# Moving the crossbar transpose of q behind the transposes of u in SyncE's queue, in a pooled-attention and mixer kernel

## The chip, the cores and the metric

The kernel runs on one core of a Trainium2 chip. The metric is device time in microseconds (us). With one core in use, the time of the slowest core is the time of that core. Before the change the kernel took 353.03 us, the median of three runs (352.23 to 353.3).

For this one-core program a run is called slow when it is over 1.5% above the fastest run of the same kernel. The ratios use fast runs only; a median is quoted over all runs of a kernel, slow ones too.

## The reference

The reference is an attention whose keys and values are averaged over groups of eight rows, followed by a mixer of two small networks. There are 8 batches, 8 heads, 576 rows and 64 columns per head.

```python
k_p = k.reshape(B, H, 72, 8, D).mean(axis=3)          # 576 keys become 72
v_p = v.reshape(B, H, 72, 8, D).mean(axis=3)
attn = softmax(scale * q @ k_p.T)                     # 576 x 72 per head
x = (attn @ v_p)  ->  (B, 576, 512)                   # heads side by side
u = x + (relu(x.T @ w_tok1) @ w_tok2).T               # token network, 576 -> 256 -> 576
out = u + relu(u @ w_ch1) @ w_ch2                     # channel network, 512 -> 1536 -> 512
```

## The kernel before

The kernel is a pipeline over batches. After a head, which does the attention and the token network of batch 0, come the *units*. Unit n is the channel network of batch n, 48 steps of two matmuls each. Between those steps the attention and token network of batch n+1 are mixed in, step by step. Unit 8 handles a ninth row block collected from all batches ("tails").

```python
LATER = {0: "kpT", 2: "o0", 3: "e0", 5: "o1", 6: "e1", 8: "o2", ...        # scores of batch n+1, from step 2
         ..., 26: "at0", 27: "at1", 30: "u0 t0", 31: "u1 t1", 32: "u2 t2", 33: "u3 t3", 34: "u4 t4"}
...
def unit(n, at):
    side = {}
    if n + 1 < B:
        load(n + 2)               # loads of k, q, v for the batch after next
        batches[n + 1][0]()       # prepare(n + 1): pooling of k and v, and the transpose of q
        side = batches[n + 1][1]
    for i, _ in enumerate(unit_steps(n, ...)):
        for s in at.get(i, "").split() if side else []:
            ... side[s]()
```

Each batch needs two kinds of crossbar transposes, both issued by SyncE. *qT* turns q of a batch (a 128 x 2560 bf16 tile, 640 KB) into the layout that the scores need. *uT* turns u (four pieces of 128 KB, steps t0 to t3, and every second batch a fifth piece for the tails) into the layout that the next channel network needs. SyncE also issues the two outputs of each of a unit's four output chunks, at steps 29, 35, 41 and 47, ahead of what else stands at that step.

```python
def load(b):
    kr = raw.tile(...); vr = raw.tile(...)                 # raw has two buffers of each
    qb = raw.tile([P, HP, BR * D + D], BF16, name="qb")
    nc.vector.memset(qb[:, :, BR * D:], 0.0)               # padding, on VectorE, for every batch
    ...                                                    # GpSimd then issues the loads of kr, qb, vr
def prepare():
    ...
    if b > 1:
        for s in ("K0", "K1", "V0", "V1"): name[s]()       # pooling, on GpSimd
    st["qT"] = att.tile([P, HP, NE, 2, BP], BF16, name="qT")
    if not first:
        nc.sync.dma_start_transpose(out=st["qT"]..., in_=qb...)
...
with tc.manual_schedule(engines={PE, POOLE}):              # TensorE and GpSimd: program order
    ...                                                    # SyncE's order is the scheduler's
```

A qb buffer is reused every second batch. Its memset, and with it the next load into it, must wait until the qT that read it has landed.

The softmax here doesn't subtract the row's maximum and nothing guards it: scores larger than these inputs give would overflow.

## Time and profile before

Starts of units are read from the timeline of TensorE: a unit starts with its first channel matmul. All unit lengths in this document are cut that way.

| us | head | unit 0 | 1 | 2 | 3 | 4 | 5 | 6 | 7, 8 and the end | span |
|---|---|---|---|---|---|---|---|---|---|---|
| before | 37.0 | 65.2 | 43.8 | 40.0 | 30.3 | 29.3 | 28.5 | 29.4 | 46.5 | 350.0 |

Units 4 to 6 are bound by TensorE, as unit 5 shows. The table of windows of the kernel before, here its line for unit 5, has for a stretch its length, then the busy time and instruction count of each engine, the granted clock, and the share of the DMA engines' time.

```profile
core 0: us, PE busy (x) PEld busy (x) DVE busy (x) ACT busy (x) POOL busy (x), PEclk, DMA share, GB/s
...
245.70:274.19 28.49, 28.34 (x180) 14.42 (x179) 15.10 (x27) 8.79 (x15) 0.00 (x0) 1.00 0.25 54
```

TensorE is busy for 28.34 of 28.49 us, at a granted clock of 1.00. A unit cannot be much shorter than this, so the time to win is the excess of units 0 to 3, some 65 us over 28.5 each (an estimate that takes unit 5 as the limit of all units).

The page gives the chain that ended last: the critical path followed back from the end, as shares of the span.

```profile
PE 64%; DMA 25%; DVE 7%; SPq 1%; issue 1%; ACT 0%; DVEq 0%; ACTq 0%
DMA qT<-qb 13%; DMA uT<-u 9%; DMA qf<-in_q_dram 2%; DVE o L366 1%; PE p_978 L361 1%; DVE x L255 1%; SPq L316 1%; DVE kTs_93 L198 1%; DVE vp L147 1%; PE p_2923 L361 1%; PE p_2329 L361 1%; PE p_2015 L361 1%; PE p_748 L361 1%; PE p_1923 L361 1
```

The chain passes for 13% of the span through waits for qT and for 9% through waits for uT. The table of waits says which engines stood still for them. The columns are engine, tile and line, what it waited for, us in total, how many times, and the longest.

```profile
PE p_803 L349 <- DMA uT<-u: 11.7, 1, 11.7
...
PE p_1436 L349 <- DMA uT<-u: 8.2, 1, 8.2
PE p_1115 L349 <- DMA uT<-u: 7.6, 1, 7.6
```

The same table for VectorE:

```profile
DVE qb L84 <- DMA qT<-qb: 28.8, 5, 15.9
```

TensorE waits 27.5 us for uT, at the starts of units 1, 2 and 3. VectorE waits 28.8 us in five memsets of qb (line 84). In that time it cannot do the work behind the memset, which TensorE needs.

Why uT is late shows in the issues. Here is SyncE's timeline of the kernel before: start, length, operation; the length is how long the issues occupied the queue.

```profile
84.94 10.66 SPq L316 DMA_TRANSPOSE uT<-u  x4
...
132.26 8.82 SPq L316 DMA_TRANSPOSE uT<-u  x4
...
208.99 5.17 SPq L316 DMA_TRANSPOSE uT<-u  x4
```

GpSimd's timeline has the loads; these two are of batch 6.

```profile
128.41 0.78 POOL L104 DMA_DIRECT2D qb<-in_q_dram  x1
129.18 0.84 POOL L91 DMA_DIRECT2D vr<-in_v_dram  x1
```

At 132.26 the four uT come right behind the loads of batch 6 (kr at 127.56 is the third), at 84.94 right behind those of batch 4 (issued from 83.05 to 85.5), and they keep the queue for 8.82 and 10.66 us. At 208.99, with no loads about, they keep it for 5.17. The landing times say the same. The list of DMA issues, cut to the window from 80 to 104 us, has what was written, the count, the size where it is known, and the median us from issue to landing:

```profile
qb<-in_q_dram POOLq DMA_DIRECT2D x1, 576.0 KB, 13.2
vr<-in_v_dram POOLq DMA_DIRECT2D x1, 576.0 KB, 16.7
uT<-u SPq DMA_TRANSPOSE x4, 12.0
```

And cut to the quiet window from 205 to 216 us:

```profile
uT<-u SPq DMA_TRANSPOSE x4, 2.4
```

A uT lands in 2.4 us when quiet and in 12.0 us beside the loads (both are medians of four). The Trainium skill gives a reason in the page "DMA: Bandwidth & Descriptors", section "Issuing engines are not separate DMA queues": DMAs started by different engines run on the same 16 DMA engines and interleave. This trace agrees, 2.4 against 12.0 us.

SyncE's timeline has seven qT, in the order of the batches: those of batches 1 to 3 from 31.8 to 73.4 us, and those of batches 4 to 7 at 111.71, 155.76, 196.25 and 224.73, each 8 to 10 us into units 1 to 4. That is two units ahead of the scores that read it. The one of batch 6, and then, in TensorE's timeline, the first scores of batch 6, in unit 5:

```profile
196.25 3.11 SPq L171 DMA_TRANSPOSE qT<-qb  x1
...
247.58 0.41 PE L232 MATMUL p_2089<-qT,kTs_92 128*72 128x256 bf16 x2 [0.15 <-DVE kTs_92 L198]
```

These scores run 1.9 us after the start of their unit and 51 us after the issue of their qT; no score waits for a qT in this kernel.

### The profile page before, as it was taken

How to read it: one execution, taken by the hardware profiler on the slowest of the kernel's cores; microseconds unless marked ns; L12 is line 12 of the kernel's file. 1: busy time of each engine (PE TensorE's matmuls, PEld its weight loads, DVE VectorE, ACT ScalarE, POOL GpSimd, SP SyncE). 2: the span in 40 equal slices, each digit the busy share in tenths (PEclk: the TensorE clock that was granted, in tenths of full speed). 3: DMA queues.
4: the chain of work that ended last, by engine and by line, in shares of the span. 5: the costliest groups of instructions: out<-in, count | busy, mean ns of one | idle time of the engine just before them, and what ended most of it. 6: DMA issues, size and time to landing. Idle time of an engine off the chain costs nothing.

```text
span 350.0 us, 4171 instructions
## 1 busy us (share of the span) xinstructions
PE 282.8 (81%) x1632; PEld 139.4 (40%) x1632; DVE 146.8 (42%) x284; ACT 86.1 (25%) x153; POOL 135.5 (39%) x120
## 2 busy tenths in 40 slices
PE   4777806839339498399937999999999999999994
PEld 1453402414115243154413544544554554444441
DVE  3245207834213354126611564465465466332331
ACT  2244602500007100072003600710620450030310
POOL 6491001699999592193805582850000000000000
PEclk9999965978959989699986999999999999999998
DMA  8999999972999929904695316225303502602214
GB/s 189 200 205 204 194 170 130 158 118 34 181 156 150 128 21 185 178 14 62 99 170 131 76 28 132 60 38 105 92 0 62 120 2 45 134 18 63 58 27 95
DMA packets 62067, 37.02 MB, mean 106 GB/s; under 512 B 40416, under 2 KB 56928, under 8 KB 62048
## 3 DMA queue, kind: packets, MB, share of 16 engines
q0 software_dynamic: 20160, 17.35, 32.6%
q1 hardware_dynamic: 41888, 19.41, 30.0%
q8 instruction: 13, 0.21, 0.2%
q14 instruction: 6, 0.05, 0.0%
HBM read 35.85 MB, written 9.44 MB: 129 GB/s over the span
## 4 chain that ended last, share of the span: by engine, by line
PE 64%; DMA 25%; DVE 7%; SPq 1%; issue 1%; ACT 0%; DVEq 0%; ACTq 0%
DMA qT<-qb 13%; DMA uT<-u 9%; DMA qf<-in_q_dram 2%; DVE o L366 1%; PE p_978 L361 1%; DVE x L255 1%; SPq L316 1%; DVE kTs_93 L198 1%; DVE vp L147 1%; PE p_2923 L361 1%; PE p_2329 L361 1%; PE p_2015 L361 1%; PE p_748 L361 1%; PE p_1923 L361 1%; PE p_2580 L361 1%
## 5 line engine op out<-in xcount | busy, mean ns | idle before, releaser
L349 PEld LDWEIGHTS <-w_ch_86 128*128 128x128 bf16 x432 | 41.1, 101 | 63.9 <-issue 32.6
L361 PEld LDWEIGHTS <-GT 128*128 128x128 bf16 x432 | 41.9, 99 | 49.0 <-issue 1.9
L245 PEld LDWEIGHTS <-ex 72*128 72x128 bf16 x320 | 15.2, 99 | 24.1 <-DVE x L255 15.4
L91 POOL DMA_DIRECT2D kr<-in_k_dram x9 | 7.5, 837 | 27.0 <-DVE t_499 L141 26.1
L193 PE MATMUL pt<-ident,kp 72*128 72x72 bf16 x64 | 4.8, 226 | 12.0 <-DVE kp L144 11.3
L84 DVE MEMSET qb<- 128x128 uint32 x8 | 1.3, 165 | 28.8 <-DMA qT<-qb 28.8
L198 DVE COPY kTs_92<-pt 64x576 bf16<-64x576 bf16 (+1 forms) x9 | 3.6, 405 | 22.9 <-PE pt L193 21.9
L349 PE MATMUL p_803<-uT,w_ch_86 128*128 128x512 bf16 x4 | 2.1, 619 | 11.7 <-DMA uT<-u 11.7
L286 PEld LDWEIGHTS <-w_tok_83 128*128 128x128 bf16 x70 | 7.4, 106 | 10.2 <-issue 3.5
L232 PEld LDWEIGHTS <-kTs_93 128*72 128x72 bf16 x64 | 7.3, 118 | 9.3 <-DVE kTs_93 L198 2.6
L232 PEld LDWEIGHTS <-kTs_92 128*72 128x72 bf16 x64 | 7.5, 122 | 8.7 <-DVE kTs_92 L198 2.1
L91 POOL DMA_DIRECT2D vr<-in_v_dram x9 | 7.3, 815 | 9.2 <-DVE t_573 L141 5.8
L193 PEld LDWEIGHTS <-kp 72*128 72x128 bf16 x64 | 4.1, 118 | 16.4 <-DVE kp L144 11.8
L304 PEld LDWEIGHTS <-w_tok_84 128*128 128x128 bf16 x64 | 6.2, 97 | 7.7 <-issue 0.5
L349 PE MATMUL p_1436<-uT,w_ch_86 128*128 128x512 bf16 x4 | 2.1, 619 | 8.2 <-DMA uT<-u 8.2
L349 PE MATMUL p_1115<-uT,w_ch_86 128*128 128x512 bf16 x4 | 2.1, 617 | 7.6 <-DMA uT<-u 7.6
L198 DVE COPY kTs_93<-pt 64x576 bf16<-64x576 bf16 (+1 forms) x10 | 3.9, 394 | 8.5 <-PE pt L193 8.4
L144 POOL TENSOR_TENSOR kp<-t_1725 72x512 bf16<-72x512 f32 x1 | 1.3, 1265 | 14.1 <-PE pt L193 14.1
L144 POOL TENSOR_TENSOR kp<-t_2044 72x512 bf16<-72x512 f32 x1 | 1.3, 1258 | 14.1 <-PE pt L193 14.1
L220 PE MATMUL pt<-ident,qb 128*128 128x128 bf16 x20 | 2.3, 262 | 5.3 <-DVE qT L222 4.7
L354 ACT ACTIVATE GT<-p_803 128x512 bf16<-128x512 f32 x1 | 0.6, 597 | 24.0 <-PE p_803 L349 24.0
L354 ACT ACTIVATE GT<-p_1436 128x512 bf16<-128x512 f32 x1 | 0.6, 597 | 22.7 <-PE p_1436 L349 22.7
(803 smaller groups left out, 703.3 us busy)
## 6 DMA issues: line engine op xcount, KB each, us to landing
out_dram<-o SPq DMA_DIRECT2D x72, 128.0 KB, 2.4
kr<-in_k_dram POOLq DMA_DIRECT2D x7, 576.0 KB, 9.1
qb<-in_q_dram POOLq DMA_DIRECT2D x7, 576.0 KB, 11.8
vr<-in_v_dram POOLq DMA_DIRECT2D x7, 576.0 KB, 15.5
w_ch_86<-in_moe_w_ch_dram POOLq DMA_DIRECT2D x3, 512.0 KB, 9.0
w_ch_87<-in_moe_w_ch_dram POOLq DMA_DIRECT2D x3, 512.0 KB, 18.7
qf<-in_q_dram SPq DMA_DIRECT2D x4, 288.0 KB, 4.1
kr<-in_k_dram POOLq DMA_DIRECT2D x2, 288.0 KB, 9.2
```

The lines of the kernel that those rows point to most:

```text
L91: nc.gpsimd.dma_start(out=t[:, h0:h1].rearrange("j h i d -> j h (i d)"), in_=src[b, h0:h1].rearrange("h (j i) d -> j h (i d)", i=POOL))
L147: eng.tensor_tensor(out=dst, in0=t4[:, 0:n, 0], in1=t4[:, 0:n, 1], op=ALU.add)
L193: nc.tensor.transpose(out=ps[:, h, :], in_=st["kp"][:, h].rearrange("j e d -> j (e d)"), identity=ident[0:SP, 0:SP])
L198: copy(out=kT[rows, half, h0 * SP:h1 * SP], in_=ps[rows, h0:h1, :].rearrange("p h j -> p (h j)"))
L232: nc.tensor.matmul(out=ps[0:SP, hl, 0:n], lhsT=kT[:, odd, h * SP:(h + 1) * SP], rhs=st["qT"][:, hp, 0:n // BP, hl, :], start=True, stop=True)
L245: nc.tensor.matmul(out=ps[:, h // 4, (h % 4) * (D + 1):(h % 4 + 1) * (D + 1)], lhsT=st["ex"][:, h * S + n0:h * S + n0 + P], rhs=st["vp"][: ...
L255: nc.vector.tensor_tensor(out=dst.rearrange("p (a h d) -> p a h d", a=2, d=D)[:, 0:na], in0=view[:, 0:na, :, 0:D], in1=den[rows, 0:na, :, ...
L286: nc.tensor.matmul(out=ps, lhsT=w_tok1[:, CHUNK[c] if c < 4 else 4 + par, m * P:(m + 1) * P], rhs=st["x"][:, c, :] if c < 4 else st["xt"], ...
L304: nc.tensor.matmul(out=ps, lhsT=w, rhs=a, start=(i == 0), stop=(i == len(mms) - 1))
L316: nc.sync.dma_start_transpose(out=dst[:, :, o:o + P], in_=src)
L349: nc.tensor.matmul(out=ps, lhsT=w_ch1[:, kk, m * P:(m + 1) * P], rhs=uT[:, kk, :], start=(kk == 0), stop=(kk == 3))
L361: nc.tensor.matmul(out=ps, lhsT=GT[:, m, c * P:(c + 1) * P], rhs=w_ch2[:, m, :], start=(m == 0), stop=(m == NM - 1))
```

## The change

qT is no longer issued at a place that the scheduler chooses. qT of batch n+2 is now issued at step 38 of unit n, behind uT of that unit and just ahead of its scores, which run from the start of unit n+1, and SyncE works in program order. The intent is that uT, which TensorE needs first, goes ahead of qT, and that qT does not hold up what follows. In unit 0, where t0 to t4 stand at steps 36 to 40, step 38 puts qT between t1 and t2.

```diff
@@ load
+        batches[b][2]["qb"] = qb
+        batches[b][2]["qT"] = att.tile([P, HP, NE, 2, BP], BF16, name="qT")
@@ prepare
-            st["qT"] = att.tile([P, HP, NE, 2, BP], BF16, name="qT")
-            if not first:
-                nc.sync.dma_start_transpose(out=st["qT"]..., in_=qb...)
@@ new
+        def qT_dma():
+            nc.sync.dma_start_transpose(out=st["qT"]..., in_=st["qb"]...)
...
+        name["qx"] = qT_dma
@@ schedule of unit 0: qT of batch 1 at step 4
-    FIRST = {8: "K0", ...
+    FIRST = {4: "qx", 8: "K0", ...
@@ unit
         for i, _ in enumerate(unit_steps(n, batches[n][2] if n < B else None)):
+            if i == 38 and n + 2 < B:
+                batches[n + 2][1]["qx"]()
...
-    with tc.manual_schedule(engines={PE, POOLE}):
+    with tc.manual_schedule(engines={PE, POOLE, SYNC}):
```

The built programs of TensorE, ScalarE and GpSimd are in the same order as before. On VectorE only the memsets of qb move: those of batch 4 and later go from the middle of units 0, 1 and 2 to the end of unit 0 and the starts of units 2, 3 and 4.

## The prediction

> **What bounds it now.** The chain of waits is 64% TensorE and 25% DMA: 13% waits for the q transpose (qT), 9% for the u transposes (uT). Cutting the span (350.0 us) where each unit's first channel matmul starts (timeline): the head takes 37.0, unit 0 65.2, units 1 to 3 43.8, 40.0 and 31.3, units 4 to 6 29.3, 28.4 and 28.7, units 7 and 8 20.7 each, the end 4.9. Units 4 to 6 are TensorE-bound (99% busy); the excess lies in units 0 to 3, about 36 + 15 + 11.5 + 3 us.
>
> Two waits make up most of it:
> - VectorE's memset of a qb buffer stands in front of work that TensorE needs, and waits until the qT that reads that buffer has landed: 15.9 us at 37.8, 1.1 at 60.5, 5.3 at 70.3, 5.2 at 116, 1.3 at 160 (waits of VectorE).
> - uT collides with the next batch's loads. In quiet units uT lands in 2.4 us and four take 5.2 us of queue; at 84.9 to 95.7, beside loads issued at 83.1 to 84.7, the median landing is 12.0 us. TensorE waits 11.7, 7.6 and 8.2 us at the starts of units 1 to 3. The Trainium skill (DMA: Bandwidth & Descriptors, "Issuing engines are not separate DMA queues") says that all queues share 16 engines; these landing times agree.
>
> **What the change does.** No work is added or removed. On SyncE, qT of batch n+2 moves to step 38 of unit n, behind uT (in unit 0 between the second and third uT). The built order shows the later memsets moved to the end of unit 0 and the starts of units 2, 3 and 4. The memset that costs 15.9 us stays, still behind the first qT (31.8 to 53.8, beside weight loads). A qb load waits for the qT that read its buffer, so two of a batch's three loads now start after uT.
>
> **Sum.** Until 60 us nothing changes. Unit 0: the 1.1 and 5.3 us waits go, plus about 2 us of slow matmuls after the second idle; then uT with qT between costs 5 to 7 us of idle: unit 1 starts near 89 instead of 102.3 (-13). Unit 1: the 5.2 and most of 7.6 us go, and slow matmuls after idles (-13). Unit 2: -9. Unit 3: -1. New cost: qT is issued about 26 us into a unit and needs 4.8 us to land when quiet, while the next scores need it at about 30; beside the kr load (22 us into the unit, after 18 us of pooling) it is later. I estimate 0 to 4 us at the starts of units 2 to 6, 6 us in all. Sum: -36 + 6 = -30: span 320; with 2 to 3 us outside it **322 us, range 310 to 334**. Faster by over 2%: 0.95; within 2%: 0.04; slower: 0.01.
>
> **In the profile.** Right if VectorE's wait for qT in the first unit stays near 16 us and the other four almost vanish; TensorE's waits for uT fall from 27.5 us to under 10; unit 0 ends near 89; units 1 to 6 take 28.5 to 33 us; the DMA share of the chain falls to about 12%; new short waits of scores or of the memset for qT at unit starts.
>
> **What would make it wrong.** qT in front of the third uT could cost unit 1's start more than 7 us. qT landing late at every unit could return the gain as a new wait. Or the loads still collide with uT.

Unit 3 is 31.3 us in that text and unit 6 is 28.7, where the table above has 30.3 and 29.4. The sum is the same.

## The result, and the profile after

| kernel | median us | lowest to highest | runs | ratio to before, 95% interval |
|---|---|---|---|---|
| before | 352.63 | 351.18 to 353.3 | 4 | |
| after | 340.72 | 340.39 to 342.8 | 4 | 0.9669 (0.9617 to 0.9721), faster |

A ratio here and below is the mean time of one kernel's fast runs over the mean of the other's fast runs in the same rounds, so it is not quite the ratio of the medians quoted beside it. The result is correct. The gain is 12 us, where 31 were predicted. The direction was right, and the time lies outside the range of 310 to 334.

| us | head | unit 0 | 1 | 2 | 3 | 4 | 5 | 6 | 7, 8 and the end | span |
|---|---|---|---|---|---|---|---|---|---|---|
| before | 37.0 | 65.2 | 43.8 | 40.0 | 30.3 | 29.3 | 28.5 | 29.4 | 46.5 | 350.0 |
| after | 38.9 | 56.3 | 31.0 | 34.8 | 35.1 | 32.8 | 33.1 | 32.6 | 46.4 | 340.9 |
| difference | +1.9 | -8.9 | -12.8 | -5.3 | +4.7 | +3.5 | +4.6 | +3.2 | 0 | -9.1 |

The head varies from 35.6 to 41.7 us over all runs without a pattern, so its +1.9 is not put down to the change. Units 0 to 2 gave 27 us. Units 3 to 6, which had been at or near TensorE's limit, gave 16 back.

The chain of the kernel after, by engine and then by line:

```profile
PE 66%; DMA 19%; DVE 7%; SPq 3%; issue 2%; another core or an unknown queue 1%; ACT 0%; DVEq 0%; ACTq 0%
DMA qT<-qb 14%; DMA uT<-u 3%; DMA qf<-in_q_dram 3%; SPq L373 1%; DVE o L370 1%; DVE x L258 1%; SPq L319 1%; DVE vp L150 1%; PE p_1366 L365 1%; PE p_2923 L365 1%; PE p_1999 L365 1%; PE p_1643 L365 1%; PE p_750 L365 1%; PE p_2549 L365 1%
```

The share of uT fell from 9% to 3%, but that of qT stayed (13% to 14%). The waits of TensorE say what qT does now; waits of 1.9 and 1.1 us for uT are left out here.

```profile
PE p_804 L353 <- DMA uT<-u: 10.2, 1, 10.2
...
PE p_2394 L235 <- DMA qT<-qb: 3.4, 1, 3.4
PE p_1457 L235 <- DMA qT<-qb: 3.0, 1, 3.0
PE p_2090 L235 <- DMA qT<-qb: 3.0, 1, 3.0
PE p_1136 L235 <- DMA qT<-qb: 2.6, 1, 2.6
PE p_1769 L235 <- DMA qT<-qb: 1.9, 1, 1.9
```

And those of VectorE after:

```profile
DVE qb L85 <- DMA qT<-qb: 30.5, 5, 16.1
```

Waits for uT fell from 27.5 to 13.2 us, of which 10.2 is the start of unit 1. But the scores (line 235) of five batches wait for qT, 13.9 us in all, where none did before. VectorE's memsets still wait (30.5 us), at other places.

SyncE's timeline shows the order that the change made. The first three lines are the end of unit 0, the next two that of unit 1 (unit 2 starts at 126.26), and the last four that of unit 4 (unit 5 starts at 228.84).

```profile
79.44 2.55 SPq L319 DMA_TRANSPOSE uT<-u  x2
82.09 4.10 SPq L225 DMA_TRANSPOSE qT<-qb  x1
86.28 2.93 SPq L319 DMA_TRANSPOSE uT<-u  x2
...
118.89 5.17 SPq L319 DMA_TRANSPOSE uT<-u  x4
...
125.44 3.14 SPq L225 DMA_TRANSPOSE qT<-qb  x1
...
220.60 5.18 SPq L319 DMA_TRANSPOSE uT<-u  x4
225.88 1.22 SPq L319 DMA_TRANSPOSE uT_tails<-u_tails  x1
227.19 1.18 SPq L373 DMA_DIRECT2D out_dram<-o  x2
228.46 3.04 SPq L225 DMA_TRANSPOSE qT<-qb  x1
```

And TensorE at the start of unit 5; the bracket gives the wait before an instruction and what ended it.

```profile
229.97 0.59 PE L353 MATMUL p_2087<-uT,w_ch_86 128*128 128x512 bf16 x2
233.58 0.38 PE L235 MATMUL p_2090<-qT,kTs_92 128*72 128x256 bf16 x2 [3.02 <-DMA qT<-qb]
...
234.73 1.91 PE L353 MATMUL p_2101<-uT,w_ch_86 128*128 128x512 bf16 x4
...
239.76 1.03 PE L353 MATMUL p_2135<-uT,w_ch_86 128*128 128x512 bf16 x4
```

qT is issued at 228.46, 0.4 us before its unit starts, because four uT (5.18 us of queue), the tail (1.22) and two outputs (1.18) stand in front of it. A quiet qT lands 5.0 us after its issue (the list of DMA issues cut to 226 to 236 us has 5.0), so at about 233.5. The scores would have run at 230.6, where TensorE had finished the matmuls of 229.97, and run at 233.58. Unit 5 loses 3.02 us there. It also loses more than the wait: the four matmuls at 234.73 take 1.91 us, four of the same shape at 239.76 take 1.03, and the granted clock from 234.7 to 237.5 is 0.50. The table of windows for units 5 and 6 shows the same loss over the whole unit.

```profile
228.84:261.89 33.05, 29.81 (x175) 14.88 (x178) 15.11 (x27) 8.89 (x15) 8.57 (x7) 0.95 0.32 66
261.89:294.48 32.59, 29.01 (x181) 14.81 (x184) 15.82 (x28) 8.79 (x15) 0.00 (x0) 1.00 0.36 76
```

In unit 5 TensorE is busy for 29.81 us at a clock of 0.95, where the same unit took 28.34 us at 1.00 before. In unit 6 the clock is 1.00, though the scores waited 3.42 us there; that unit loses the wait alone.

The gain of unit 1 shows on GpSimd, whose loads of qb and vr (here those of batch 5) now wait for the later qT:

```profile
131.01 0.78 POOL L107 DMA_DIRECT2D qb<-in_q_dram  x1 [19.42 <-DMA qT<-qb]
131.78 0.83 POOL L94 DMA_DIRECT2D vr<-in_v_dram  x1
```

They start at 131, behind the four uT of 118.89, which therefore take 5.17 us of queue and land in 2.4 us. Before, GpSimd had issued these loads of batch 5 at 104.3 and 105.0 and had run on, so that those of batch 6 stood at 128.4 and 129.2, in front of the uT of 132.26, which took 8.82. Now those of batch 6 start at 150.6.

### The profile page after: what moved, and what is told of

Its sections match the earlier page's. It is cut to its first block, busy times and chain, and to the rows that moved or that the text cites. A ratio compares the mean times of both kernels' runs of the same rounds, so it can differ in the third digit from the quotient of the medians.

```text
span 340.9 us, 4143 instructions
## 1 busy us (share of the span) xinstructions
PE 281.7 (83%) x1601; PEld 140.2 (41%) x1632; DVE 147.5 (43%) x284; ACT 86.5 (25%) x153; POOL 135.4 (40%) x120
## 3 DMA queue, kind: packets, MB, share of 16 engines
q1 hardware_dynamic: 41888, 19.41, 29.4%
## 4 chain that ended last, share of the span: by engine, by line
PE 66%; DMA 19%; DVE 7%; SPq 3%; issue 2%; another core or an unknown queue 1%; ACT 0%; DVEq 0%; ACTq 0%
DMA qT<-qb 14%; DMA uT<-u 3%; DMA qf<-in_q_dram 3%; SPq L373 1%; DVE o L370 1%; DVE x L258 1%; SPq L319 1%; DVE vp L150 1%; PE p_1366 L365 1%; PE p_2923 L365 1%; PE p_1999 L365 1%; PE p_1643 L365 1%; PE p_750 L365 1%; PE p_2549 L365 1%
## 5 line engine op out<-in xcount | busy, mean ns | idle before, releaser
L107 POOL DMA_DIRECT2D qb<-in_q_dram x7 | 5.4, 776 | 53.4 <-DVE qb L85 28.3
L235 PEld LDWEIGHTS <-kTs_93 128*72 128x72 bf16 x64 | 7.6, 124 | 18.0 <-issue 12.2
L85 DVE MEMSET qb<- 128x128 uint32 x8 | 1.3, 165 | 30.5 <-DMA qT<-qb 30.5
L235 PEld LDWEIGHTS <-kTs_92 128*72 128x72 bf16 x64 | 8.0, 130 | 15.8 <-issue 10.0
L192 PEld LDWEIGHTS <-kp 72*128 72x128 bf16 x64 | 3.7, 109 | 16.2 <-DVE kp L147 12.1
L353 PE MATMUL p_804<-uT,w_ch_86 128*128 128x512 bf16 x3 | 1.6, 618 | 10.4 <-DMA uT<-u 10.2
L219 PEld LDWEIGHTS <-qb 128*128 128x128 bf16 x20 | 1.7, 118 | 8.4 <-issue 6.1
L205 PEld LDWEIGHTS <-ident 72*72 72x72 bf16 x32 | 4.7, 148 | 0.8 <-issue 0.2
```

Source lines behind the costliest of these rows:

```text
L107: nc.gpsimd.dma_start(out=qb[:, :, 0:BR * D], in_=q_in(0, HP))
L192: nc.tensor.transpose(out=ps[:, h, :], in_=st["kp"][:, h].rearrange("j e d -> j (e d)"), identity=ident[0:SP, 0:SP])
L205: nc.tensor.matmul(out=ps[0:SP, 0:HP * D], lhsT=ident[0:SP, 0:SP], rhs=st[t][:, hs, i, :], start=(i == 0), stop=(i == POOL - 1))
L219: nc.tensor.transpose(out=ps[:, rr].rearrange("m l p -> m (l p)"), in_=st["qb"][:, hp, rr * P:(rr + 1) * P], identity=ident)
L235: nc.tensor.matmul(out=ps[0:SP, hl, 0:n], lhsT=kT[:, odd, h * SP:(h + 1) * SP], rhs=st["qT"][:, hp, 0:n // BP, hl, :], start=True, stop=True)
L353: nc.tensor.matmul(out=ps, lhsT=w_ch1[:, kk, m * P:(m + 1) * P], rhs=uT[:, kk, :], start=(kk == 0), stop=(kk == 3))
```

## The experiments

Eleven changed kernels, one of them twice, ran in three groups. Each group shared its runs of the kernel before (medians 352.55, 352.54 and 351.77 us, seven runs each). All gave results within the tolerance. Four theories were at stake; the letters in the expectations stand for theories of this kind:

- The late qT gives the gain back. It lies behind uT and two outputs, and the scores of the next unit want it at once.
- The memsets of qb on VectorE, which still wait for qT, give it back.
- In unit 0 the loads of batch 4, not the place of qT, hold uT up.
- The program order of SyncE is by itself what gains.

### 1. Scores that don't wait for qT: stale_scores

This kernel is wrong: from batch 2 on the scores read the qT of batch 1, kept in a tile of its own. All transposes are still issued. The result still passed the tolerance, since the weights of this attention are nearly uniform, but it is not a solution.

```diff
-  rhs=st["qT"][:, hp, 0:n // BP, hl, :]
+  rhs=(st if b < 2 else batches[1][2])["qT"][:, hp, 0:n // BP, hl, :]
-  batches[b][2]["qT"] = att.tile(..., name="qT")
+  batches[b][2]["qT"] = (singles if b == 1 else att).tile(..., name="qT" if b != 1 else "qT1")
```

> The changed kernel, wrong on purpose: the scores of batches 2 to 7 read batch 1's qT, so TensorE no longer waits for the late transposes; these are still issued in the same places, and VectorE's memsets still wait for them. Theory A (the gain is given back because qT lands 3 us after the scores of units 2 to 6 need it): the five waits of TensorE (13.9 us) go, and with them 1 to 2 us of slow matmuls after each; units 5 and 6 fall from 33.1 and 32.6 us to below 30, the median from 340.7 to about 320. Rival B (the memset in front of VectorE's evictions is the wait that costs): units keep 32 to 33 us, since the third PSUM buffer is still held until the memset is through, median 335 or more.

Measured: 327.86 us (327.23 to 328.74), ratio 0.9292 (0.9236 to 0.9347). Units 4 to 6 took 30.7, 28.5 and 29.3 us, which is TensorE's limit again for 5 and 6. The memset waits of VectorE were still 30.3 us. So the late qT costs the changed kernel 13 us (340.7 less 327.9). That is a net figure: the waits for qT that went sum to 13.9 us, while two waits for uT grew from 1.1 and 1.9 to 3.3 and 3.7. No memset of qb that waits lies in units 5 and 6, so the memsets did not hold these. The time is 8 us longer than the 320 that was expected. Waits for uT remained, as the waits of TensorE show:

```profile
PE p L353 <- DMA uT<-u: 16.7, 3, 9.6
```

The longest is at the start of unit 1. Two of 3.3 and 3.7 us are at the starts of units 3 and 4, where a load of kr was issued among or just behind the four uT (at 148.31, uT from 145.32; at 182.00, uT from 179.84).

### 2. The padding written once, in the changed kernel: memset_once_after

Two lasting qb buffers are padded once, so no later memset can wait for qT.

```diff
-  qb = raw.tile([P, HP, BR * D + D], BF16, name="qb")
-  nc.vector.memset(qb[:, :, BR * D:], 0.0)
+  qb = qbs[b % 2]
+  if b < 2:
+      nc.vector.memset(qb[:, :, BR * D:], 0.0)
+  qbs = [singles.tile([P, HP, BR * D + D], BF16, name=f"qb{i}") for i in range(2)]   # once
```

> The changed kernel with two lasting qb buffers, zero padded once, so VectorE never waits for a qT. Theory A: nothing changes in units 2 to 6 (33 to 35 us each), as TensorE itself waits for qT there; in unit 0 VectorE no longer idles 16 us, so the pooling of batch 1 is done before qT lands, and unit 0 falls from 56.3 us by 4 to 8. Median 332 to 337. Rival B: units 4 to 6 fall to below 30 us and the median to 322 or less.

Measured: 335.58 us (333.96 to 336.7), ratio 0.9493 (0.9425 to 0.9562). VectorE waits for no qT any more. The scores still wait for qT by 2.6, 3.1, 1.7, 3.0 and 3.4 us in units 2 to 6, which took 34.7, 36.5, 30.8, 33.0 and 34.2 us. A sixth wait, of 10.3 us, is new: in unit 0 the memset had waited 16.1 us for the first qT, and now the scores wait for it themselves. So the memsets cost the changed kernel about 5 us, and they are not what lengthened units 3 to 6.

### 3 and 4. The padding written once, in the kernel before: memset_once_before and memset_once_before_2

The same edit in the kernel before, to see what the memset waits alone are worth.

> The kernel before with two lasting qb buffers, zero padded once; SyncE's order as before. It tells how much of the change's gain is the memset's wait (16 + 1 + 5 + 5 + 1 us of VectorE) and how much the collision of the u transposes with the loads. Theory A: unit 0 loses the first wait and the 5 us one, unit 1 the 5 us one, but TensorE's waits for uT at the starts of units 1 to 3 (27.5 us together) stay within 6 us; median 333 to 340. Rival (the memset is all there is): the uT waits shrink as well and the median falls to below 328.

Measured: 330.61, 346.09, 348.25 and 346.75 us. Against the one run at 330.61 the other three counted as slow. The profile fell in the 330.61 run. It was repeated:

> The run memset_once_before again: it gave 330.6 us once and 346 to 348 three times, and no profile of the longer kind. If the kernel has two courses, both come again, near 331 and 347; with the longer one profiled, it is to be seen in which unit the 16 us are. If the short one was a chance, all runs lie at 345 to 349.

Measured: 345.64 us (344.71 to 346.75), ratio 0.9826 (0.978 to 0.9873), which leaves open whether it is 2% faster. The short course did not come again, so the expectation that both would be seen missed. The two profiles differ by 16.2 us of span, and unit 0 by 12.0 (47.4 and 59.4). TensorE's timeline has the first channel matmul of unit 1, in the short course:

```profile
86.49 0.59 PE L351 MATMUL p<-uT,w_ch 128*128 128x512 bf16 x2 [1.44 <-DMA uT<-u]
```

And in the long course:

```profile
99.64 1.01 PE L351 MATMUL p<-uT,w_ch 128*128 128x512 bf16 x2 [18.94 <-DMA uT<-u]
```

In the long course uT is 18.94 us late at the start of unit 1, and its three waits for uT sum to 37.9 us, more than the 27.5 of the kernel before. In unit 0 the scores wait 7.6 us for the first qT, where the memset had waited. So removing the memset waits alone is worth 1.7%: what they had cost turns into waits for qT and for uT beside the loads. In the short course the wait for uT is 1.44 us. The two traces show where they part. In the short course the four uT of unit 0 are issued from 79.46, ahead of the loads of batch 4 (from 84.88), and keep the queue for 5.67 us; in the long course the loads start at 80.52, just ahead of the uT at 80.78, which keep it for 9.16 us. The loads come later in the short course because the first qT landed later (the scores ran at 60.70 instead of 56.34). This is read from one trace of each; the short course was seen once in eight runs.

### 5. qT earlier: qT_early

qT is issued at step 20 from unit 1 on. In SyncE's queue this puts it right behind the last outputs of the unit before, ahead of uT.

```diff
-  if i == 38 and n + 2 < B:
+  if i == (20 if n else 38) and n + 2 < B:
```

> The changed kernel with qT of batch n+2 placed at step 20 of unit n instead of 38, for n of 1 and up: ahead of the outputs and of uT in SyncE's queue, which is idle there. Theory A: the five waits of the scores for qT vanish, units 4 to 6 fall to about 28.5 us each; but the loads, no longer held back by a late qT, run into uT again, so that TensorE waits 5 to 8 us for uT at the starts of two of the units 2 to 4. Median 322 to 332. Rival (units 2 to 6 are long because of loads held back to the unit's start, which compete there): units 5 and 6, which have no loads left before and after, stay at 32 us or more.

Measured: 325.16 us (321.78 to 327.13), ratio 0.9181 (0.9095 to 0.9268). Units 4 to 6 took 29.3, 28.5 and 29.3. SyncE's timeline in unit 4 (191.03 to 220.38):

```profile
193.15 3.25 SPq L225 DMA_TRANSPOSE qT<-qb  x1
...
212.13 5.17 SPq L319 DMA_TRANSPOSE uT<-u  x4
```

qT of the next batch is issued at 193.15, 27 us before its unit starts, and again at 222.55. No score waits for qT. This is the late qT removed with a correct kernel, and it gains 15.6 us over the changed kernel (medians of all runs; one of the four counted as slow). The page "DMA: Bandwidth & Descriptors" of the Trainium skill, section "Rules for kernel authors", advises to issue a DMA early and wait for it late; 325 against 341 us agrees. The waits for uT of 5 to 8 us that were expected at the starts of two of units 2 to 4 did not come (1.2 us at one of them). The one at the start of unit 1, whose qT had not been moved, stayed (9.8 us). Instead the memsets wait 3.9 to 6.7 us in units 1 to 3, which took 33.3, 30.2 and 35.1 us.

### 6. qT of unit 0 in front of all uT: unit0_qT_first

```diff
-  if i == 38 and n + 2 < B:
+  if i == (38 if n else 30) and n + 2 < B:
```

> The changed kernel with one qT moved: that of batch 2, in unit 0, from between the second and the third uT to ahead of the first (step 30, SyncE's queue is idle there). Theory A (the third and fourth uT are late because that qT takes 4.1 us of the queue in front of them, and so fall beside the next loads): TensorE's wait for uT at the start of unit 1 falls from 10.2 to 3 to 5 us, the median from 340.7 to 334 to 336, units 2 to 6 stay at 33 to 35 us. Rival C (uT is late there because of the loads of batch 4 at 85 us alone, which now all three start then): the wait stays at 8 us or more, median 338 or more.

Measured: 340.87 us, but one run took 334.8 and the other three, 340.4 to 342.5, counted as slow against it. In the profile, taken in one of the three (342.53 us), the wait for uT at the start of unit 1 is 9.0 us, against 10.2. Moving qT from between the uT to in front of them does not take the wait away in that run: the loads of batch 4, from 82.85, meet the last uT, issued at 83.2, which lands 9.7 us later. Since the run counted as slow, this stays a hint.

### 7. Both earlier: both_early

Experiments 5 and 6 in one kernel (step 20, and step 30 in unit 0).

> qT at step 20 in units 1 and up, as in the run qT_early, and at step 30 in unit 0. If the two losses are separate they add: median 325.2 less 5 to 7, so 318 to 321. If loads of batch 4 then start sooner and collide with uT, nothing is gained: 324 or more.

Measured: 324.98 us (322.97 to 328.9), ratio 0.9195 (0.9121 to 0.9269). It is the same as qT_early alone; the 318 to 321 us that were hoped for did not come. The profile, from the one run that counted as slow, has a wait for uT of 8.9 us at the start of unit 1, again with loads (from 84.59) behind and among the uT (from 81.00).

### 8. Both earlier, and the padding once: both_early_memset_once

> As both_early, with two lasting qb buffers padded once, so that VectorE never waits for a qT. The waits of VectorE that qT_early still has (13.2 us in unit 0, 4.6, 3.9 and 6.7 us in units 1 to 3) go: units 1 to 3 fall from 33.3, 30.2 and 35.1 us to 29 to 31, unit 0 by 4 us more; median 305 to 313. Rival (without the memset's brake the loads run ahead into uT, as in the kernel before): uT waits of 7 to 9 us come back at the starts of two units, median 316 or more.

Measured: 314.88 us (311.44 to 319.62), ratio 0.8895 (0.8817 to 0.8972). The waits for uT are 4.0 and 4.4 us, the scores of unit 0 wait 6.6 us for the first qT, and units 3 to 6 took 28.5, 29.3, 28.5 and 29.4. With qT early the memsets are worth about 10 us (324.98 less 314.88), against 5 with qT late; the intervals of the four ratios are too wide to call these two different. The median is 2 us above the expected range.

### 9. Program order alone: order_only

The kernel before, with SyncE put in program order and nothing else.

```diff
-  with tc.manual_schedule(engines={PE, POOLE}):
+  with tc.manual_schedule(engines={PE, POOLE, SYNC}):
```

> The kernel before with SyncE in program order and nothing else changed: qT of batch n+1 is then issued at the very start of unit n, behind the last output of unit n-1, and needed two steps later. Theory A: the scores wait for qT in every unit from 1 on, 4 to 5 us each, as qT needs 5 us to land, so units 4 to 6 take 33 to 35 us like in the changed kernel; median 342 to 350. Rival D (the program order itself is the gain and the late qT of no account): units 4 to 6 below 30 us and a median below 335.

Measured: 360.02 us (357.29 to 362.11), ratio 1.0203 (1.013 to 1.0276): slower, but whether by 2% is unclear. Program order by itself gains nothing. qT now stands behind all outputs of the unit before, at the moment of its use. SyncE's timeline has qT 1.4 us behind the start of unit 4 (203.56):

```profile
205.00 3.04 SPq L172 DMA_TRANSPOSE qT<-qb  x1
```

TensorE's timeline has the first scores of that unit, and slow matmuls behind them:

```profile
210.13 0.61 PE L233 MATMUL p<-qT,kTs 128*72 128x256 bf16 x2 [4.85 <-DMA qT<-qb]
...
211.92 1.92 PE L350 MATMUL p<-uT,w_ch 128*128 128x512 bf16 x4
```

The waits of TensorE have the sum:

```profile
PE p L233 <- DMA qT<-qb: 35.7, 6, 8.5
```

The scores wait for qT in six units, 35.7 us in all, and units 3 to 6 take 36.5 to 39.7 us. The expectation had the direction and the waits, but not the size (342 to 350 us). Against this kernel, taking qT from behind all the outputs to step 38 is worth 19 us (360.0 to 340.7). The waits for uT, though, are already down to 5.6 us here: with qT behind uT, and the loads of qb and vr behind that qT (at 96.72 in unit 1, 133.42 in unit 2), uT is clear, and the scores pay for it.

### 10. qT of unit 0 behind all uT: unit0_qT_last

```diff
-  if i == 38 and n + 2 < B:
+  if i == (38 if n else 41) and n + 2 < B:
```

> The changed kernel with one qT moved: that of batch 2, in unit 0, from between the second and the third uT to behind the last (step 41). Theory A (that qT in front holds the third and fourth uT up by 4.1 us): they are issued near 82 to 85 us, and TensorE's wait for uT at the start of unit 1 falls from 10.2 to 4 to 6 us, partly given back as a wait of 2 to 4 us of the first scores for qT; median 336 to 340. Rival C (the loads of batch 4 at 85 us are the cause): the wait for uT stays at 8 us or more; median 340 to 345.

Measured: 341.4 us (338.83 to 342.59), ratio 0.968 (0.9617 to 0.9744), the same as the changed kernel. Two lines of TensorE's timeline show an exchange:

```profile
84.44 0.59 PE L353 MATMUL p<-uT,w_ch 128*128 128x512 bf16 x2 [1.44 <-DMA uT<-u]
...
94.31 0.61 PE L235 MATMUL p<-qT,kTs 128*72 128x256 bf16 x2 [8.15 <-DMA qT<-qb]
```

uT is only 1.44 us late for unit 1, which starts at 84.44 instead of 95.25. Then the scores wait 8.15 us for qT, issued at 85.81 beside the load of kr, and unit 1 takes 40.2 us instead of 31.0. The edit moves more than qT: the load of qb waits for this qT, so that the loads of qb and vr of batch 4 start at 94.75 instead of 91.09, and only that of kr (82.81) is beside the uT.

### 11. Loads behind the pooling: loads_after_pooling

GpSimd issues the loads of batch n+2 after the pooling of batch n+1, from unit 2 on. GpSimd runs ahead of TensorE, so this takes the loads of batch 4 from the end of unit 0 on TensorE, 85 to 93 us, to 101 us.

```diff
+  if n < 2:
       load(n + 2)
   batches[n + 1][0]()
+  if n >= 2:
+      load(n + 2)
```

> The changed kernel with one order on GpSimd reversed from unit 2 on: the loads of batch n+2 are issued behind the pooling of batch n+1 instead of ahead of it, so that the loads of batch 4 start near 103 us and not at 85; SyncE and VectorE keep their orders. Rival C (those loads are what makes the last uT of unit 0 late): TensorE's wait for uT at the start of unit 1 falls from 10.2 to 2 to 5 us although the qT still stands in front, median 330 to 336. Theory A (the qT in front is): the wait stays at 6 us or more and the median at 338 or more. Units 2 to 6 keep their waits of 2 to 3.5 us for qT in both.

Measured: 339.95 us (336.34 to 343.29), ratio 0.9629 (0.9557 to 0.9701). The wait for uT at the start of unit 1 falls to 4.7 us, with qT still between the uT:

```profile
88.07 0.73 PE L353 MATMUL p<-uT,w_ch 128*128 128x512 bf16 x2 [4.74 <-DMA uT<-u]
```

The four uT land in 3.6 us or less here. So more than half of unit 0's wait needs the loads, in the one profile. But a wait of 7.2 us for qT appears in unit 4 (38.8 us long), and the median misses the 330 to 336 that were expected.

### 12. All together: early_once_loads_later

Step 20, and 30 in unit 0; padding once; loads behind the pooling from unit 2 on.

> The run both_early_memset_once with the loads behind the pooling as in loads_after_pooling. If loads beside uT are what is left (waits of 4.0 and 4.4 us at the starts of units 1 and 2), these fall below 1.5 us each, units 0 and 1 by 4 us each, and the median goes from 314.9 to 304 to 310. If the later loads come too late for pooling, new waits for kp or vp appear in units 3 to 5 and the median stays at 313 or more.

Measured: 311.71 us (310.33 to 318.61), ratio 0.8848 (0.8797 to 0.8898). This is the fastest kernel, and correct; it is 11.5% below the kernel before. Its interval overlaps that of experiment 8, so the later loads are not shown to be worth anything here. It misses the expected 304 to 310. Its waits for uT are 1.9 and 5.2 us, and the scores of unit 0 wait 8.3 us for the first qT; the load of batch 4 at 97.4 us now runs into the uT of unit 1 instead.

### The units side by side

| us | head | unit 0 | 1 | 2 | 3 | 4 | 5 | 6 |
|---|---|---|---|---|---|---|---|---|
| before | 37.0 | 65.2 | 43.8 | 40.0 | 30.3 | 29.3 | 28.5 | 29.4 |
| after | 38.9 | 56.3 | 31.0 | 34.8 | 35.1 | 32.8 | 33.1 | 32.6 |
| order_only | 37.2 | 48.9 | 40.8 | 37.0 | 39.7 | 37.0 | 36.8 | 36.5 |
| stale_scores | 36.0 | 56.9 | 31.0 | 33.1 | 33.6 | 30.7 | 28.5 | 29.3 |
| qT_early | 40.1 | 52.3 | 33.3 | 30.2 | 35.1 | 29.3 | 28.5 | 29.3 |
| both_early_memset_once | 41.7 | 43.7 | 34.2 | 30.5 | 28.5 | 29.3 | 28.5 | 29.4 |
| early_once_loads_later | 38.5 | 43.2 | 33.8 | 31.7 | 28.5 | 29.4 | 28.5 | 29.3 |

## Why the prediction was wrong

The prediction was right that the change makes the kernel faster, and where the gain would come from. It was wrong in the size: 341 instead of 322. Of the 20.9 us by which the span exceeds the predicted 320, 14.7 lie in units 2 to 6, 4.1 in unit 0, 1.9 in the head and 0.2 in unit 1.

- **What bounds the kernel before.** The reading held. Units 0 to 3 carried the excess, through memsets that wait for qT and uT beside loads.
- **Unit 1, predicted -13.** Measured -12.8. The four uT had the DMA engines nearly to themselves (5.17 us of queue instead of 8.82), because GpSimd, held for 19.4 us by the later qT, issued the loads of batch 5 at 131 us and those of batch 6 from 150.6 us on.
- **Unit 0, predicted -13.** Measured -8.9. The wait for uT at the start of unit 1 was put at "5 to 7 us"; it was 10.2. Experiments 10 and 11 share it out: with qT behind the uT it is 1.4 (there two of the three loads start later too), with the loads later and qT still between the uT it is 4.7, each in one profile. So in these profiles about 5 us are left without the loads, and the rest comes from the loads; that the loads are enough by themselves, even with qT in front of all uT, is what the profiles of experiments 6 and 7 suggest (9.0 and 8.9 us, both in runs that counted as slow).
- **Units 2 to 6: the step that failed.** The prediction wrote: "New cost: qT is issued about 26 us into a unit and needs 4.8 us to land when quiet, while the next scores need it at about 30 [...] I estimate 0 to 4 us at the starts of units 2 to 6, 6 us in all." The mechanism was named, and it is the one that came; the term was mis-sized. Experiment 1 measures it at 13 us net, and experiment 5, with qT issued earlier, gains 15.6. In unit 1, the only one of these that did not itself begin with a wait for qT, qT is issued 30.2 us into the unit (125.44 less 95.25), not 26: the uT begin at 23.6, and they and two outputs fill the queue for 6.5 us. (The kernel before suggests where the 26 came from: uT begin 21.1 us into its unit 4, and four take 5.2 us. The two outputs (1.2 us of queue) and, every second unit, the tail (1.2 us) seem to have been left out; this is an estimate.) In units 2 to 5 it is issued between 1.7 us and 0 us before the next unit starts, and the scores want it some 1.7 us after that start. The landing time was right (4.8 predicted, 5.0 measured). So the scores waited 1.9 to 3.4 us in every one of five units, 13.9 us in all, and after some of these waits the matmuls were slow for a while on top (unit 5: 1.5 us more of busy TensorE).
- **The rest of the miss in units 2 to 6.** The sum for these units was 153.5 (157.5 before, less 9 and 1, plus 6) and they took 168.2, so 14.7 more. Seven of it is 13 instead of 6 for the late qT, by experiment 1. The other 7.7 is there even without the wait for qT: in experiment 1 these units took 155.2, where the prediction without its new cost has 147.5. Two waits for uT, of 3.3 and 3.7 us beside a load of kr, lie in it. That the loads of kr are what delays these uT is argued from their times and was not tried by itself.
- **"The other four almost vanish".** The memset waits of VectorE did not vanish; they sum to 30.5 us over five. The one of 7.1 us at the end of unit 0 moved to where it is hidden; those at the starts of units 2, 3 and 4 (2.5, 3.0 and 1.9 us) lie beside the wait of the scores for the same qT. Experiment 2 puts all the memsets in the changed kernel at 5 us.
- **DMA's share of the chain, predicted 12%.** Measured 19%, since the chain now goes through qT at the starts of the units. "Waits for uT under 10" was 13.2.
- **What would make it wrong.** All three risks that the prediction listed came true in part: qT in front of the third uT cost more than 7 us, qT landed late in every unit, and one set of loads still met uT.

In short, the later qT held back the loads that wait for it, which cleared uT's way, and it took memset waits out of units 0 and 1 (of 1.1, 5.3 and 5.2 us); together units 0 to 2 gained 27 us. The change paid with qT behind everything, where it had been two units early, which costs 3 to 5 us in each of the units 3 to 6, where there had been no excess to spend. Experiment 5 gets the first without the second.

## What to carry to other kernels

A transfer that is moved back in a queue must be costed by what stands in front of it: add up the queue time of those issues and compare the landing with the step that needs it, in every unit and also in those that had no waits before. A wait of an engine in front of a buffer's reuse (here a memset of padding) is best removed by removing its need, but what it is worth depends on the next wait in line: here it was 1.7% (6 us) in the kernel before, 5 us in the changed one and 10 us once qT was early, and in each case a part came back as a wait of the scores for the same qT. Move the big transfer to a stretch where the queue and the DMA engines are idle, here right behind the previous unit's outputs (3.25 us of queue in unit 4, but 10.1 in unit 1, where loads were about), instead of only behind the urgent one.

## What the Trainium skill lacked or had wrong

- "DMA: Bandwidth & Descriptors" (section "Latency and other measured facts") gives a DMA transpose an effective bandwidth of 261 GB/s in one kernel, with a non-contiguous middle dimension, and 350 to 400 GB/s for the contiguous case, but no time from issue to landing for small tiles. Here the 640 KB qT landed 5.0 us after issue when quiet, 131 GB/s (655,360 bytes over 5.0 us), and the 128 KB uT in 2.4 us. The 261 GB/s alone would give 2.5 us for qT (an estimate from that page), half the time. The two sizes together give some 200 GB/s for the added 512 KB and a fixed part of about 1.75 us (an estimate from two points), so at these sizes the bandwidth alone does not give the time.
- The same page has cycles of the sequencer for transposes of other sizes (a table of hardware before and after trn3 B0), but not how long a transpose of these sizes keeps the queue on trn2, nor that loads lengthen this. Here it was 1.2 to 1.3 us per 128 KB uT and 3.04 us for the 640 KB qT when quiet, and 10.66 us for four uT beside loads.
- "TensorE: Matmul & The Clock Gate" (section "Part 1: The HAM clock gate") has the clock fall to half after at least one idle window of about 3.4 us, and calls the window free-running. Here a wait of TensorE of 3.02 us was followed by matmuls at nearly half speed (four in 1.91 us instead of 1.03; granted clock 0.50 from 234.7 to 237.5), and a wait of 3.42 us in the next unit was not (four of the same shape in 1.03; clock 1.00). That a wait's effect depends on its place fits the free-running window; that 3.02 us can be enough does not fit the figure, as far as the modelled end of the matmul before the wait can be trusted.
